# An attention block with a gated MLP on one core: 32-bit back transposes, residual by accumulating DMAs, a fifth shift tile, DMA transposes from SP for tokens 512 to 2047, and a new planned order

## The chip, the cores and the metric

The kernel runs on 1 core of one Trainium2 chip. The metric is the device time in microseconds (us) of one execution; three runs of the kernel before gave 658.18 us as median (658.02 to 658.38).

## The reference, cut to what matters

```python
def reference(A_x, A_wq, A_wk, A_wv, A_wo, B_x, B_w1, B_w2):
    xn = _layernorm(x)                      # x: 2048 tokens x 512
    q = (xn @ wq) as 32 heads of 16;  k = xn @ wk;  v = xn @ wv      # one k and one v for all heads
    p = _softmax(q @ k.T * 16 ** -0.5)      # 32 heads x 2048 x 2048
    s = (p @ v, heads side by side) @ wo    # 2048 x 512
    g = _silu(_silu(xn @ w1) @ w2)          # 2048 x 1792, then 2048 x 512
    return x + s * g
```

B_x of the inputs is not used. Data are bfloat16.

## The kernel before, in words

**Tiles.** The 2048 tokens are four chunks of 512. A score tile is 128 x 512: 64 keys of one chunk, for two heads, against 512 queries, written by four matmuls into one of the eight PSUM banks. A group g (0 to 31) is 64 such tiles (32 blocks of 64 keys, two halves i of a q tile); 2,048 score tiles in all. A score tile is exponentiated in one of two ways:
- by ACT with the Exp function (L1674), one bank or two banks in one instruction, into `pa_sb`;
- by DVE, which writes the bits of an approximate power of two as uint16 (L1042) into `db_sb`, in batches of eight tiles. Three shifted copies of the batch follow in `ds_sb`, each one integer addition over 128 x 4096 (POOL, L1225; in a few cases DVE, L1221), and the four versions are multiplied with differently weighted values `v_sb`, so that their sum approximates the exponential.

PE multiplies each with V (L1303) and adds up in a bank per group. `make_norm` then transposes the bank in 32 x 32 blocks in place (L1320), takes the reciprocal of the sum (L1323), multiplies into `otr_sb` (L1325), and for each pair of groups transposes back, as bfloat16, into `on_sb` (L1335).

**Jobs.** Between the score tiles PE runs jobs that share the banks: q (xn @ wq), h (xn @ w1, tanh on ACT at L761 and a gate on DVE at L762), z (u @ w2, the same two steps into `tmp_sb`) and w (the `on_sb` tiles @ wo). After a w job DVE multiplies with `tmp_sb` in the bank (L814) and adds x from `xr_sb` into `ob_sb` (L817); SP loads `xr_sb` (L825) and stores `ob_sb` (L809). The last four token tiles have a tail of their own (L798 to L803, L1554 to L1568).

**Prologue.** x arrives in 16 tiles of 128 tokens; DVE takes mean and variance (L539, L543), a reciprocal square root and writes `xn_sb` (L568, four slots). PE transposes it through PSUM (L607, by `mk_T`) and DVE copies to `xnT_sb` (L618; the first two tiles by ACT and in halves). For each chunk then follow K (L633 on PE, L651 on DVE into `kt_sb`), a POOL DMA that shifts `kt_sb` for odd groups (L1349), and V (L670, L679). A score tile needs K of its chunk, and its PV needs V of its chunk. DVE tiles start only when K of all 16 token tiles is there (`pick_d`).

**What sets the order.** All instructions are placed at build time by `Planner`, which keeps a clock for every engine and appends the instruction that it picks to that engine's list. Each engine runs its list strictly in order and waits on semaphores. `s_step` picks between an ACT tile and a DVE tile by the work that each engine has ahead; a batch of DVE tiles is only opened while a group has `MARGIN` tiles left. A table of random seeds (`SEEDS`), one for each 6 us stretch of the planner's clock, varies these thresholds. `xn_sb` tile t and t + 4 share a slot, so tile t + 4 is only written when tile t was read. `ports=2` marks operations of DVE and POOL that share a port and are kept apart by semaphores.

Of the kernel before, what the change touches and what calls it, by code (L numbers as in the profile page):

```python
# [8 lines left out]
ALU = mybir.AluOpType  # L9
# [13 lines left out]
SEEDS, STRETCH = [0, 0, 882634, 0, 348373, 328499, 78780, 554384, 89101, 903077, 320169, 0, 878569, 280070, 102111, 381856, 427096, 265022, 0, 740569, 0, 0, 0, 191854, 393933, 374197, 266972, 0, 665170, 0, 882882, 218695, 9227, 955074, 159633, 731624, 518155, 138034, 620799, 357599, 376984, 365473, 457970, 796664, 668429, 641664, 991272, 0, 0, 23990, 593814, 88565, 504692, 394759, 276845, 267858, 882770, 104810, 721623, 135503, 603776, 0, 337714, 100793, 638616, 0, 419715, 752789, 751312, 664693, 308960, 0, 762547, 276261, 218757, 897693, 0, 624478, 290921, 0, 713781, 335568, 417921, 100939, 814701, 0, 180062, 99721, 614963, 258262, 411291, 131548, 802432, 314922, 883804, 569039, 54637, 401726, 110613, 0, 983842, 914345, 0, 0, 0, 0, 0, 0, 0, 0], 6000.0  # L23
# [32 lines left out]
NPA, NDB, NDS, NTM = 27, 3, 4, 4  # L56
MARGIN, MARGIN_END = 17, 20
# [10 lines left out]
MATE = 176.663  # L68
RH, EVR, SC_PRIO, PES = 0, (0, 2, 3), 0, (1, 0)
# [26 lines left out]
class Planner:  # L96

    def __init__(self):
# [7 lines left out]
        self.held = None  # L106
# [3 lines left out]
        self.last2 = {DV: None, PO: None}  # L110

# [68 lines left out]
    def tensor(self, mode, lane, dur, emit, reads, writes, t, after=None, n=8, held=None):  # L180
# [18 lines left out]
        if both or lane == 1:  # L199
            self.held = held  # L200
# [18 lines left out]
    def avail(self, task):  # L219
# [5 lines left out]
        if task.eng == PO and task.ports == 2:  # L225
            for d in self.tasks[DV]:
                if d.ports == 2 and d.gate is None and all(p.op is not None for p in d.preds) and (
                        self.ready(DV, d.reads, d.writes) <= self.clk[PO] + HOLD_PO):
                    return None
# [25 lines left out]
    def finalize(self, new_sem):  # L255
# [96 lines left out]
def bass_recurrent_scan__grouped_kv_mqa__dense_activation_silu__prompt_kernel(  # L352
# [29 lines left out]
    with ExitStack() as es:  # L382
# [59 lines left out]
        xv = xf.rearrange("(t p) d -> p t d", p=P)  # L442

# [53 lines left out]
        pl.add(Task(PO, 1800.0, lambda g: g.memset(kt_sb[0:DH, 1, :], 0.0), [("xn", 3)], [("kt1", c) for c in range(NC)], 3,  # L497
                    gate=lambda: all(xn_task[t].op is not None for t in range(4)), ports=2))
# [99 lines left out]
        def mk_T(tiles, bk=None):  # L598
# [12 lines left out]
            def consume(jb, op):  # L611
# [9 lines left out]
                preds=[xn_task[t] for t in tiles], bk=bk, mode="F")  # L621

# [156 lines left out]
        def mk_z(tt, pace):  # L779
            c, r = divmod(tt, 4)  # L780

            def consume(jb, op):
# [3 lines left out]
                tmp_task[tt] = gated(b, k, 0.25, tmp_sb[:, tt % NTM, :], ("tmp", tt % NTM))  # L786
# [8 lines left out]
        def scaled(tt, b, r=None):  # L795
            k = tt % 2
            if r in EVR:
                ev = pl.add(Task(AC, 490.0, lambda a: a.activation(xn_sb[:, r, :], bank(b), ACT.Copy, scale=0.25),  # L798
                                 [("ps", b)], [("xn", r)], 0))
                fin_task[tt] = Task(DV, 333.0, lambda v: v.tensor_tensor(xn_sb[:, r, :], xn_sb[:, r, :], tmp_sb[:, tt % NTM, :], ALU.mult),  # L800
                                    [("xn", r), ("tmp", tt % NTM)], [("xn", r)], SC_PRIO, [ev, tmp_task[tt]], ports=2)
# [3 lines left out]
                [("ps", b), ("tmp", tt % NTM)], [("fin", k)], 0 if r is None else SC_PRIO, [tmp_task[tt], fin_task.get(tt - 2) if r is None or r - 2 not in EVR else None])  # L805
# [6 lines left out]
        def final(tt, b):  # L812
            k = tt % 2
            t1 = Task(DV, T_P, lambda v: v.scalar_tensor_tensor(  # L814
                out=bank(b), in0=bank(b), scalar=0.25, in1=tmp_sb[:, tt % NTM, :], op0=ALU.mult, op1=ALU.mult),
                [("ps", b), ("tmp", tt % NTM)], [("ps", b)], 0, [tmp_task[tt]])
# [7 lines left out]
        def add_xr(tt):  # L824
# [958 lines left out]
```

## Time and profile before

| | |
|---|---|
| median of three runs | 658.18 us (658.02 to 658.38) |
| span of the profiled execution, first to last instruction | 656.6 us |
| busy: PE, ACT, DVE, POOL | 648.1, 640.4, 639.3, 571.0 us |
| instructions: ACT, DVE, POOL | 1128, 1170, 320 |
| granted TensorE clock | 1.000 |
| DMA share of 16 engines, queue of SP | 6.3% |

The span runs from the first to the last instruction; the page gives no other time for the profiled execution, so 658.18 - 656.6 = 1.6 us is taken as what lies around it. Busy time is the union of the instructions' durations: an instruction that starts while the one before it still drains adds only what is not overlapped, so an engine that shows 100% may still have waited a little between starts. Lines of the kernel are named L followed by the number.

### The profile page before, as it was taken

To read this page: it belongs to the slowest core of one execution; us is meant where nothing else is said; L and a number is where in the kernel's file an instruction comes from. 1 tells how busy PE (TensorE), PEld (TensorE's weight loads), DVE (VectorE), ACT (ScalarE), POOL (GpSimd) and SP (SyncE) were. 2 spreads that over 40 slices of the span, in tenths; PEclk is the share of its full clock that TensorE was granted. 3 is DMA by queue.
4 is the path that set the end of the run, shared out by engine and by line. 5 is a ranking of instruction groups with operands and counts; after the bars stand their busy time and mean duration, and the time that the engine had idled before them with its cause. 6 is when DMAs were issued, how large, how long until landed. Compare 5 with 4: busy or idle time off the path is not lost.

```text
span 656.6 us, 44475 instructions
## 1 busy us (share of the span) xinstructions
PE 648.1 (99%) x22180; PEld 330.7 (50%) x19436; DVE 639.3 (97%) x1170; ACT 640.4 (98%) x1128; POOL 571.0 (87%) x320
## 2 busy tenths in 40 slices
PE   8999999999999999999999999999999999999997
PEld 4445554544455554554555454444555555554444
DVE  8999999999999999999999999999999999999976
ACT  6889999999999999999999999999999999999995
POOL 4038899999998978999999878999999999889991
PEclk9999999999999999999999999999999999999999
DMA  6311111000011100000000010000000000100001
GB/s 177 129 48 42 42 28 29 10 4 10 5 35 28 35 28 4 10 4 6 9 4 12 20 36 26 4 5 9 5 10 4 10 21 20 35 11 5 4 4 34
DMA packets 13641, 15.92 MB, mean 24 GB/s; under 512 B 2320, under 2 KB 12816, under 8 KB 13456
## 3 DMA queue, kind: packets, MB, share of 16 engines
q1 hardware_dynamic: 12976, 12.36, 6.3%
q8 instruction: 162, 2.65, 1.7%
q0 software_dynamic: 192, 0.46, 0.2%
q10 hardware_dynamic: 288, 0.26, 0.1%
q14 instruction: 23, 0.19, 0.1%
HBM read 8.95 MB, written 2.10 MB: 17 GB/s over the span
## 4 chain that ended last, share of the span: by engine, by line
PE 84%; ACT 10%; DVE 3%; POOL 1%; DMA 0%; issue 0%
PE ps L967 28%; PE ps L1303 23%; PE ps L705 20%; PE ps L961 13%; ACT pa_sb L1674 9%; ACT t_sb L761 1%; DVE stats_sb L539 1%; DVE xn_sb L568 1%; PE ps L1514 1%; DVE xnT_sb L618 0%; DMA kt_sb<-kt_sb 0%; POOL qt_sb L501 0%; POOL kt_sb L497 0%; DVE v_sb L679 0%; DVE kt_sb L651 0%
## 5 line engine op out<-in xcount | busy, mean ns | idle before, releaser
L1674 ACT ACTIVATE pa_sb<-ps 128x512 bf16<-128x512 f32 (+1 forms) x1038 | 611.0, 771 | 4.1 <-PE ps L967 3.8
L1225 POOL INT64_ADD ds_sb<-db_sb x300 | 562.1, 1896 | 41.5 <-DVE db_sb L1042 31.9
L1042 DVE TENSOR_SCALAR db_sb<-ps 128x512 uint16<-128x512 f32 x808 | 499.9, 680 | 4.2 <-PE ps L961 2.0
L967 PE MATMUL ps<-qt_sb,kt_sb 64*32 64x512 bf16 x5448 | 470.6, 378 | 1.5 <-DVE v_sb L679 0.8
L1303 PE MATMUL ps<-ds_sb,v_sb 64*32 64x512 bf16 x4848 | 350.5, 377 | 0.0
L1303 PE MATMUL ps<-pa_sb,v_sb 64*32 64x512 bf16 x2480 | 269.9, 377 | 0.5 <-DVE v_sb L679 0.5
L961 PE MATMUL ps<-qt_sb,kt_sb 64*32 64x512 bf16 x2744 | 263.6, 375 | 0.0
L967 PEld LDWEIGHTS ps<-qt_sb,kt_sb 64*32 64x32 bf16 x5448 | 130.4, 89 | 162.8 <-ACT pa_sb L1674 70.6
L1303 PE MATMUL ps<-db_sb,v_sb 64*32 64x512 bf16 x1616 | 210.6, 377 | 0.0
L1303 PEld LDWEIGHTS ps<-ds_sb,v_sb 64*32 64x32 bf16 x4848 | 133.4, 91 | 43.5 <-issue 15.0
L705 PE MATMUL ps<-xnT_sb,w_sb 64*32 64x512 bf16 x1792 | 134.6, 377 | 0.0
L705 PE MATMUL ps<-w_sb,u_sb 64*32 64x512 bf16 x1792 | 133.5, 376 | 0.0
L1303 PEld LDWEIGHTS ps<-pa_sb,v_sb 64*32 64x32 bf16 x2480 | 91.4, 91 | 26.8 <-issue 7.9
L1303 PEld LDWEIGHTS ps<-db_sb,v_sb 64*32 64x32 bf16 x1616 | 66.5, 91 | 15.7 <-issue 5.3
L705 PEld LDWEIGHTS ps<-xnT_sb,w_sb 64*32 64x32 bf16 x1792 | 42.8, 91 | 24.9 <-issue 6.7
L705 PEld LDWEIGHTS ps<-w_sb,u_sb 64*32 64x32 bf16 x1792 | 44.4, 91 | 20.3 <-issue 6.2
L761 ACT ACTIVATE t_sb<-ps 128x512 bf16<-128x512 f32 x72 | 49.1, 682 | 0.0
L762 DVE SCALAR_TENSOR_TENSOR u_sb<-t_sb,ps 128x512 bf16<-128x512 bf16 x56 | 37.9, 677 | 1.0 <-ACT t_sb L761 1.0
L705 PE MATMUL ps<-xnT_sb,wq_sb 64*32 64x512 bf16 x480 | 37.1, 377 | 0.0
L705 PE MATMUL ps<-wo_sb,on_sb 64*32 64x512 bf16 x384 | 30.2, 377 | 0.0
L1320 DVE STREAM_TRANSPOSE ps<-ps 128x512 f32<-128x512 f32 (+1 forms) x33 | 23.2, 706 | 3.6 <-PE ps L1303 3.6
L1349 POOL DMA_DIRECT2D kt_sb<-kt_sb x4 | 2.3, 566 | 21.3 <-DVE rstd_sb L559 7.8
(78 smaller groups left out, 193.0 us busy)
## 6 DMA issues: line engine op xcount, KB each, us to landing
xr_sb<-in_A_x_dram SPq DMA_DIRECT2D x16, 128.0 KB, 2.4
out_dram<-ob_sb SPq DMA_DIRECT2D x16, 128.0 KB, 1.8
w_sb<-in_B_w_dram SPq DMA_DIRECT2D x1, 1792.0 KB, 7.3
w_sb<-in_B_w_dram SPq DMA_DIRECT2D x14, 128.0 KB, 2.1
ds_sb<-in_A_x_dram SPq DMA_DIRECT2D x3, 512.0 KB, 7.1
qt_sb<-qt_sb SPq DMA_DIRECT2D x16, 96.0 KB, 2.2
wq_sb<-in_A_wq_dram SPq DMA_DIRECT2D x1, 512.0 KB, 5.4
wo_sb<-in_A_wo_dram SPq DMA_DIRECT2D x4, 128.0 KB, 2.9
```

What stands on the lines that cost most here:

```text
L539: ts_ = pl.add(Task(DV, 593.0, lambda v, t=t: v.bn_stats(stats_sb[:, t, :], x_tile(t)), [xkey(t)], [("st", t)], 1 + j, gate=(lambda j=j: S ...
L568: xn_task[i] = pl.add(Task(DV, 323.0, lambda v, i=i: v.tensor_scalar(xn_sb[:, i % 4, :], x_tile(i), mv_sb[:, i, 0:1], rstd_sb[:, i:i + 1], ...
L705: h = pe.matmul(bank(b)[32 * j:32 * (j + 1), :], lhsT=lhs(k, rows, 32 * j, 32), rhs=rhs(k, rows), start=first, stop=last, tile_position=(r ...
L761: t1 = Task(AC, T_AF + 0.8333 * NQ, lambda a: a.activation(t_sb[:, k, :], bank(b), ACT.Tanh, scale=scale), [("ps", b)], [("t", k)], 0)
L762: t2 = Task(DV, T_P, lambda v: v.scalar_tensor_tensor(out=dst, in0=t_sb[:, k, :], scalar=1.0, in1=bank(b), op0=ALU.add, op1=ALU.mult), [(" ...
L961: h = pe.add_instruction(mybir.InstMatmult(name=pe.bass.get_next_instruction_name(), engine=mybir.EngineType.PE, ins=[pe.lower_ap(q), pe.l ...
L967: h = pe.matmul(to, lhsT=keys, rhs=q, start=True, stop=True, tile_position=(r0, 32 * j), skip_group_check=True)
L1042: bt.P[k] = pl.add(Task(DV, T_P, lambda v: v.tensor_scalar(db_sb[:, bt.b, k * NQ:(k + 1) * NQ], bank(b), 128.0 * LOG2E, 128.0 * (SHIFT_BET ...
L1225: whole["po"].append(pl.add(Task(PO, T_P64, lambda g: g.int64_add(ds_sb[:, s, :].bitcast(U64), db_sb[:, bt.b, :].bitcast(U64), words), rea ...
L1303: h = pe.matmul(bank(OB)[q:q + 32, :], lhsT=lhs[rows], rhs=rhs[rows], start=s0, stop=s1, tile_position=(64 * l, q), skip_group_check=True)
L1320: t1 = pl.add(Task(DV, (T_TR - 60.0) / parts + 60.0, lambda v, cols=cols: v.transpose(bank(OB)[:, cols], bank(OB)[:, cols]), [("ps", OB)], ...
L1674: op = pl.place(AC, 0.8333 * NQ * n + T_AF, lambda a: a.activation(pa3[:, k0:k1 + 1:max(1, k1 - k0), :], ps3[:, b0:b1 + 1:step, :], ACT.Ex ...
```

## The change

- **Back transposes**: the transpose into `on_sb` reads and writes pairs of bfloat16 as one 32-bit element (256 elements a row in place of 512). `make_norm` writes `otr_sb` in another layout for it, and the readers of `on_sb` take every second column (`on_cols`).
- **Residual**: for token tiles 0 to 11, x is copied to the output by a DMA from HBM to HBM (SP), the multiplication with `tmp_sb` writes `ob_sb`, and a DMA from POOL adds `ob_sb` to the output. The DVE addition is gone for these twelve. The last four tiles keep theirs.
- **DMA transposes**: tokens 512 to 2047 are transposed from `xn_sb` to `xnT_sb` by 48 DMA transposes of 128 x 128 from SP, four for each token tile, that count on one semaphore per tile. The PE transposes and DVE copies of these tokens are gone.
- **Buffers**: `tmp_sb` is now `xn_sb`; `xr_sb`, `fin_sb` and a new `fx_sb` lie in `w1_sb`, once it is no longer read; the room goes to a fifth `ds_sb` tile.
- **Planner**: DVE tiles may start with K of 12 token tiles (`DK`), rank behind the prologue until it is over (`PRO_PRIO`); two DVE tiles that are ready together may become one instruction (`both_passes`); POOL's port operations also give way to gated DVE tasks (`YIELD`); `MARGIN` 17 to 24; new `SEEDS`. Among the other new names, `P_HIGH` keeps a batch from being opened while POOL has much shift work ahead; the score tiles still go to one lane of PE and the PV products to the other.

```diff
-NPA, NDB, NDS, NTM = 27, 3, 4, 4
-MARGIN, MARGIN_END = 17, 20
+NPA, NDB, NDS, NTM = 27, 3, 5, 4
+MARGIN, MARGIN_END = 24, 20
...
+TR32, XBAR, T_TURN = 1, 1, 500.0
+YIELD, W_LATE = 1, 0.0
+DK, PRO_PRIO, ZDMA = 12, 6, 0
...
+        def add_turn(t):
+            cols = slice(t * P, (t + 1) * P)
+            for d in range(NDC):
+                def emit(e, d=d):
+                    return e.dma_start_transpose(xnT_sb[:, d, cols], xn_sb[:, t % 4, d * P:(d + 1) * P])
+                last = d == NDC - 1
+                pl.add(Task(SP, T_TURN, emit, [("xn", t % 4)], [("xnT", t)] if last else [], 0,
+                            [xn_task[t]], dma=1, on_place=(lambda op: t_done.add(t)) if last else None)).ring = f"x{t}"
...
         def final(tt, b):
-            k = tt % 2
+            if tt < NT - 4:
+                t1 = Task(DV, T_P, lambda v: v.scalar_tensor_tensor(
+                    out=ob_sb[:, tt % 4, :], in0=bank(b), scalar=0.25, in1=tmp_sb[:, tt % NTM, :], op0=ALU.mult, op1=ALU.mult),
+                    [("ps", b), ("xn", tt % NTM)], [("ob", tt % 4)], 0, [tmp_task[tt], out_task.get(tt - 4)])
+                fin_task[tt] = t1
+                out_task[tt] = pl.add(Task(PO, T_SWDGE, lambda e: e.dma_start(ov[:, tt, :], ob_sb[:, tt % 4, :], accum_op=ALU.add),
+                                           [("ob", tt % 4)], [("out", tt)], 0, [t1, xr_task[tt]], dma=256 * 1024, on_place=outs.append))
+                return t1,
...
         def add_xr(tt):
+            if tt < NT - 4:
+                xr_task[tt] = pl.add(Task(SP, 60.0, lambda e: e.dma_start(ov[:, tt, :], xv[:, tt, :]),
+                                          (), [("out", tt)], 2, [], dma=256 * 1024))
...
-            mk_T([4 * c, 4 * c + 1])
-            mk_T([4 * c + 2, 4 * c + 3])
+            if XBAR:
+                for t in range(4 * c, 4 * c + 4):
+                    add_turn(t)
...
-            if st["assigned"] < 8 or any(k not in evac_kt or evac_kt[k].op is None for k in range(NKT)):
+            if st["assigned"] < 8 or any(k not in evac_kt or evac_kt[k].op is None for k in range(DK)):
...
+                op = pl.place(DV, one.dur + NQ / 0.96, lambda v: v.tensor_scalar(
+                    db3[:, k0:k1 + 1:k1 - k0, :], ps3[:, b0:b1 + 1:b1 - b0, :], 128.0 * LOG2E, 128.0 * (SHIFT_BETA + 127.0),
...
-                t2_task[oi] = pl.add(Task(DV, (T_TR - 60.0) / parts + 60.0, lambda v, cols=cols: v.transpose(
+                t2_task[oi] = pl.add(Task(DV, (T_TR - 60.0) / parts / (2 if TR32 else 1) + 60.0, lambda v, cols=cols: v.transpose(
+                    on_sb[:, oi % NON, cols].bitcast(FP32), otr_sb[:, oi % 2, cols].bitcast(FP32)) if TR32 else v.transpose(
                     on_sb[:, oi % NON, cols], otr_sb[:, oi % 2, cols]),
```

The counts of the planned instructions, before and after: ACT exponentials of one bank 836 and 844, of two banks 202 and 198 (1,240 tiles in both); DVE tiles 808 in both (798 single instructions and 5 of two after); shifts on POOL 300 and 298, on DVE 3 and 5; PV matmuls 8,944 in both; score tiles that reuse the loaded weights 686 and 633; PE transposes 64 and 16; DVE copies of `xnT_sb` 8 and 2; DMAs on POOL 4 and 16.

Three places show how the order moves. The first is SP's list around the load of w1 (`w_sb<-in_B_w_dram`, 128x4x1792); before:

```order
L445 DMA ds_sb<-in_A_x_dram 128x4x512 x3
L715 DMA qt_sb<-qt_sb 96x512
L445 DMA w_sb<-in_B_w_dram 128x4x1792
L445 DMA w_sb<-in_B_w_dram 128x512 x4
L715 DMA qt_sb<-qt_sb 96x512
```

and SP's list at the same place after the change:

```order
L468 DMA ds_sb<-in_A_x_dram 128x4x512 x3
L756 DMA qt_sb<-qt_sb 96x512
L468 DMA w_sb<-in_B_w_dram 128x4x1792
L659 DMA_TRANSPOSE xnT_sb<-xn_sb 128x128 x48
L468 DMA w_sb<-in_B_w_dram 128x512 x4
L756 DMA qt_sb<-qt_sb 96x512
```

All 48 transposes stand behind the load of w1 and ahead of the first w2 tiles and of the next q copy.

The second is DVE's list in the prologue, with the semaphores that a row waits for (q_ and an engine: that engine's progress; ax and a number: the four DMA transposes of that token tile). Before, where tokens 512 to 1023 are normalized:

```order
L565 SCALAR_TENSOR_TENSOR rstd_sb<-var_sb,rstd_sb 128x4 [waits q_DVE]
L679 TENSOR_TENSOR v_sb<-ps,wj_sb 128x5x8x16 [waits q_PE]
L568 TENSOR_SCALAR xn_sb<-ds_sb,mv_sb,rstd_sb 128x512 [waits q_DVE,q_POOL]
L568 TENSOR_SCALAR xn_sb<-ds_sb,mv_sb,rstd_sb 128x512 x3
L539 BN_STATS stats_sb<-ds_sb 128x6 [waits d12]
L618 COPY xnT_sb<-ps 128x4x256 [waits q_PE] x2
```

and after, from the end of the normalization of tokens 1024 to 1535 to K of tokens 512 to 1023:

```order
L597 SCALAR_TENSOR_TENSOR rstd_sb<-var_sb,rstd_sb 128x4 [waits q_DVE]
L600 TENSOR_SCALAR xn_sb<-ds_sb,mv_sb,rstd_sb 128x512 [waits ax4,q_DVE]
L600 TENSOR_SCALAR xn_sb<-ds_sb,mv_sb,rstd_sb 128x512 [waits ax5]
L600 TENSOR_SCALAR xn_sb<-ds_sb,mv_sb,rstd_sb 128x512 [waits ax6]
L600 TENSOR_SCALAR xn_sb<-ds_sb,mv_sb,rstd_sb 128x512 [waits ax7]
L571 BN_STATS stats_sb<-ds_sb 128x6 [waits d25]
L571 BN_STATS stats_sb<-ds_sb 128x6
L692 TENSOR_SCALAR kt_sb<-ps,part_sb 128x512 [waits q_PE]
```

The copies are gone, and each normalized tile of the next chunk now waits for the DMA transposes of the tile whose slot it takes.

The third is PE's list around K of tokens 512 to 1023 (`xnT_sb,wke_sb`, 32x512, x16). Before, with the PE transposes (`ident,xn_sb`) ahead of it, 20 score tiles stand ahead of K in the whole list:

```order
L607 MATMUL ps<-ident,xn_sb 128x128 x8
L1303 MATMUL ps<-pa_sb,v_sb 32x512 x4
L607 MATMUL ps<-ident,xn_sb 128x128 x8
L1303 MATMUL ps<-pa_sb,v_sb 32x512 x4
L967 MATMUL ps<-qt_sb,kt_sb 32x512 x4
L1303 MATMUL ps<-pa_sb,v_sb 32x512 x4
L961 MATMUL ps<-qt_sb,kt_sb 32x512 x4
L1303 MATMUL ps<-pa_sb,v_sb 32x512 x4
L967 MATMUL ps<-qt_sb,kt_sb 32x512 x4
L1303 MATMUL ps<-pa_sb,v_sb 32x512 x4
L961 MATMUL ps<-qt_sb,kt_sb 32x512 x4
L633 MATMUL ps<-xnT_sb,wke_sb 32x512 x16
```

and after:

```order
L1024 MATMUL ps<-qt_sb,kt_sb 32x512 x4
L1018 MATMUL ps<-qt_sb,kt_sb 32x512 x4
L1024 MATMUL ps<-qt_sb,kt_sb 32x512 x4
L746 MATMUL ps<-xnT_sb,w_sb 32x512 x4
L1018 MATMUL ps<-qt_sb,kt_sb 32x512 x4
L746 MATMUL ps<-xnT_sb,w_sb 32x512 x8
L674 MATMUL ps<-xnT_sb,wke_sb 32x512 x16
L746 MATMUL ps<-xnT_sb,w_sb 32x512 x4
L1024 MATMUL ps<-qt_sb,kt_sb 32x512 x4
L1018 MATMUL ps<-qt_sb,kt_sb 32x512 x4
```

K of the second chunk moved from behind 20 score tiles to behind 30 of the 32 that the first chunk allows in groups 0 and 1; K of the third from behind 36 to behind 44, and K of the fourth from behind 47 to behind 64, of which 8 are DVE tiles.

More of the change, by code (lines that the diff above doesn't have):

```diff
@@ L226, in avail @@
             for d in self.tasks[DV]:
-                if d.ports == 2 and d.gate is None and all(p.op is not None for p in d.preds) and (
-                        self.ready(DV, d.reads, d.writes) <= self.clk[PO] + HOLD_PO):
+                if d.ports == 2 and (d.gate is None or YIELD and self.clk[DV] <= self.clk[PO] + HOLD_PO and d.gate()) and all(
+                        p.op is not None for p in d.preds) and self.ready(DV, d.reads, d.writes) <= self.clk[PO] + HOLD_PO:
                     return None
@@ L309, in finalize @@
                     op.sem, op.val = sems[e], n
+        for e in ENGINES:
+            for op in self.order[e]:
+                if op.ring is not None:
+                    op.val = rings[op.ring][1]
     def run_engine(self, e, handle):
@@ L1247, in pv_half @@
             got, soon, old = {}, INF, INF
+            last = ob_last.get(g)
+            turn = pl.vis(last, PE) if last is not None and last.lane != lane else 0.0
             for i in range(2):
                 for ent in pvq[g][i]:
+                    if ent.lane != lane:
+                        continue
                     c = ent.reads[-1][2]
@@ L1263, in pv_half @@
             return t, got
-        ob = {}
+        ob, ob_last = {}, {}
         def take_ob():
@@ L1305, in emit @@
                 return h
-            pl.tensor("U", 0, MM, emit, sorted(reads, key=str), [("ps", OB)], t, n=4 * len(mm))
+            last = ob_last.get(g)
+            ob_last[g] = pl.tensor("U", lane, MM, emit, sorted(reads, key=str), [("ps", OB)], t, n=4 * len(mm),
+                                   after=last if last is not None and last.lane != lane else None)
             make_shifts()
@@ L1693, in generic_step @@
             now, soon = pl.best(e, t)
+            if now is not None and now[1].slot is not None and both_passes(max(t, now[2]), now[1]):
+                return True
             if now is not None:
```

214 lines of the change are left out of this document (150 added, 64 removed).

## The prediction

> **What bounds the kernel now.** First the busy times of the page and their course over the span, then a table by stage.
>
> ```profile
> PE 648.1 (99%) x22180; PEld 330.7 (50%) x19436; DVE 639.3 (97%) x1170; ACT 640.4 (98%) x1128; POOL 571.0 (87%) x320
> ACT  6889999999999999999999999999999999999995
> 20.00:40.00 20.00, 18.40 (x510) 9.03 (x446) 17.91 (x51) 16.48 (x29) 1.58 (x3) 1.00 0.29 104
> 40.00:640.00 600.00, 599.88 (x21052) 306.65 (x18396) 593.44 (x1021) 599.90 (x1060) 559.39 (x299) 1.00 0.06 17
> 640.00:657.00 17.00, 12.56 (x324) 6.67 (x284) 10.89 (x22) 9.54 (x15) 2.68 (x2) 1.00 0.10 33
> ```
>
> The columns of the last three rows are PE, PEld, DVE, ACT, POOL. From 40 to 640 us ACT shows 599.90 of 600, DVE 593.44, POOL 559.39. So ACT is the bound, with DVE close behind; ACT's idle time lies before 40 and after 640. Whether ACT is really back to back needs its cadence, since its instructions overlap.
>
> ```profile
> L1674 ACT ACTIVATE pa_sb<-ps 128x512 bf16<-128x512 f32 x836 | 446.2, 694 | 2.6 <-PE ps L967 2.4
> L1674 ACT ACTIVATE pa_sb<-ps 128x1024 bf16<-128x1024 f32 x202 | 213.7, 1090 | 1.5 <-PE ps L967 1.4
> L761 ACT ACTIVATE t_sb<-ps 128x512 bf16<-128x512 f32 x72 | 49.1, 682 | 0.0
> 52.31 4.02 ACT L1674 ACTIVATE pa_sb<-ps 128x512 bf16<-128x512 f32 x8
> 56.13 0.69 ACT L761 ACTIVATE t_sb<-ps 128x512 bf16<-128x512 f32 x1
> 11.51 14.23 ACT L1674 ACTIVATE pa_sb<-ps 128x512 bf16<-128x512 f32 x24 [0.50 <-PE ps L967]
> 633.77 13.21 ACT L1674 ACTIVATE pa_sb<-ps 128x1024 bf16<-128x1024 f32 x17
> ```
>
> One bank lasts 694 ns, but eight of them, all of one bank, start between 52.31 and 56.13: 3.82 / 8 = 0.478 us from start to start, and the rest overlaps. The last row is 11 instructions of two banks and 6 of one: (13.21 - 6 x 0.478 - 0.2 for the drain) / 11 = 0.92 us per two banks. The work of ACT is then 836 x 0.478 + 202 x 0.92 + 72 x 0.478 = 619.8 us. It runs from 11.51 to 646.98 us, 635.3 without the drain. So ACT lost 15.5 us after its first exponential. The view of ACT in order of time shows where 3.3 of them are:
>
> ```profile
> 26.45 4.14 ACT L1674 ACTIVATE pa_sb<-ps 128x1024 bf16<-128x1024 f32 x7 [0.71 <-PE ps L967]
> 31.45 1.57 ACT L1674 ACTIVATE pa_sb<-ps 128x512 bf16<-128x512 f32 x3 [0.86 <-PE ps L967]
> 33.73 2.64 ACT L1674 ACTIVATE pa_sb<-ps 128x1024 bf16<-128x1024 f32 x3 [0.70 <-PE ps L967]
> 38.83 8.80 ACT L1674 ACTIVATE pa_sb<-ps 128x512 bf16<-128x512 f32 x16 [1.05 <-PE ps L967]
> ```
>
> The bracket is idle time and what ended it: scores that came late in the prologue. 599.90 leaves 0.1 for the steady part, so some 12.1 us are **hidden waits**, shorter than the overlap of two instructions. After 646.98 comes the tail, 9.6 us.
>
> **The change, part by part.** The sum is made against the profiled execution: span 656.6 us, and 658.18 - 656.6 = 1.6 us around it.
>
> *ACT's own work.* 1,240 tiles before and after, 844 x 0.478 + 198 x 0.92 + 34.4 = 620.0 us: **+0.2**. This is the main point: no part of the change takes work from the bounding engine. What it can gain is ACT's 15.5 lost us and the tail.
>
> *DVE.*
>
> ```profile
> 619.28 10.99 DVE L1042 TENSOR_SCALAR db_sb<-ps 128x512 uint16<-128x512 f32 x18
> L817 DVE TENSOR_TENSOR ob_sb<-ps,xr_sb 128x512 bf16<-128x512 f32 x12 | 8.1, 677 | 0.0
> L618 DVE COPY xnT_sb<-ps 128x1024 bf16<-128x1024 bf16 x6 | 4.0, 680 | 0.5 <-PE ps L607 0.5
> L1335 DVE STREAM_TRANSPOSE on_sb<-otr_sb 128x512 bf16<-128x512 bf16 x15 | 10.5, 702 | 0.0
> L1320 DVE STREAM_TRANSPOSE ps<-ps 128x256 f32<-128x256 f32 x2 | 0.8, 444 | 1.5 <-PE ps L1303 1.5
> L1221 DVE TENSOR_SCALAR ds_sb<-db_sb 128x4096 uint16<-128x4096 uint16 x3 | 3.5, 1222 | 0.0
> ```
>
> Eighteen evictions take 10.99 us, 0.61 from start to start, 0.07 less than their mean of 0.68. By it 12 additions go (12 x 0.60 = 7.2) and 6 copies (3.6). A transpose of 256 32-bit elements is in the trace at L1320, 444 ns against 702: 15 x 0.26 = 3.9, and 0.3 for the two halves in the tail. Two more shifts on DVE cost 2 x 1.15 = 2.3. Two DVE tiles in one instruction are not in the trace: between nothing and one whole eviction saved, 5 x 0 to 0.61; I take the overhead that ACT saves, 2 x 0.478 - 0.92 = 0.04 each, nearly nothing. DVE loses 12.7 us net, all of it beside ACT. It is worth something only where PE waited for DVE to free a bank and so fed ACT late:
>
> ```profile
> PEld ps L967 <- ACT pa_sb L1674: 70.6, 292, 0.5
> PEld ps L967 <- DVE db_sb L1042: 35.7, 165, 0.4
> ```
>
> The waits of the score tiles' weight loads for a bank are 35.7 / 106.3 = 34% DVE's. Of the 12.1 hidden us that is 4.1. DVE stays over 95% busy, so I take three quarters: **-3.1**. The ends are 0 (ACT itself is what frees banks late) and -4.1; past it, all 12.1.
>
> *Prologue.*
>
> ```profile
> 16.50 1.38 DVE L568 TENSOR_SCALAR xn_sb<-ds_sb,mv_sb,rstd_sb 128x512 bf16<-128x512 bf16 x4 [0.76 <-POOL kt_sb L497]
> 17.27 22.11 SPq L445 DMA_DIRECT2D w_sb<-in_B_w_dram  x5
> 19.73 1.05 PE L633 MATMUL ps<-xnT_sb,wke_sb 128*32 128x512 bf16 x16
> 21.51 0.73 DVE L651 TENSOR_SCALAR kt_sb<-ps,part_sb 128x512 bf16<-128x512 f32 x1
> 0.75 0.86 SPq L445 DMA_DIRECT2D ds_sb<-in_A_x_dram  x2
> 50.31 0.52 SPq L715 DMA_DIRECT2D qt_sb<-qt_sb  x1
> w_sb<-in_B_w_dram SPq DMA_DIRECT2D x1, 1792.0 KB, 7.3
> qt_sb<-qt_sb SPq DMA_DIRECT2D x16, 96.0 KB, 2.2
> ```
>
> In the new list the normalized tiles 4 to 7 stand ahead of V and of POOL's fill, so they come at about 14.6 us in place of 16.50. SP then issues w1 (15.4, done at 15.9) and the 48 transposes. No DMA transpose is in the trace. The nearest rows are single DMAs on SP: 0.43 us each for x, 0.52 for the copy inside SBUF, which lands 2.2 us after issue. I take 0.5 per transpose, its end 1.7 after. The far end is a queue that holds each until it has landed, 2.2 each; the near end 0.43. With 0.5, K's inputs are there at 15.9 + 8 + 1.7 = 25.6 us for the second chunk, 33.6 for the third, 41.6 for the fourth. From K's start to scores I count 1.05 + 0.73 + 0.6 for three handovers = 2.4 us: scores at 28.0, 36.0, 44.0. ACT's first 32 tiles (18 single, 7 double) end at 11.5 + 15.0 = 26.5, so it waits 1.5 us plus its hand-over; 14 tiles later 36.0 comes as ACT runs out; 12 ACT tiles after that (8 of the 20 are DVE's) end near 42. That is 4 to 5 us of waits, as before (3.3 shown and about 1 hidden): **0**. Each 0.1 us more per transpose costs 4.8 us, since PE's list holds K of the fourth chunk ahead of everything that follows; DVE waits as well, its next normalized tile standing in its list ahead of statistics, K and V. The w1 transfer fills the same queue until about 22.7 us (7.3 from issue), which the issue of the first chunk's transposes covers. Their PE counterparts (48 transposes, some 3.7 us) and PSUM banks go; PE's list waits for K anyway: 0.
>
> The Trainium skill, "VectorE: DVE Perf Modes", section "The three transpose paths", puts a 128 x 128 bf16 transpose through the DMA crossbar at 1309 ns, against 390 on TensorE. No run here shows it yet. If that were the time per transpose in one queue, the sum would be an estimated 48 x 0.81 = 39 us higher; the same skill, "Advanced Engine Details and Errata", section "X-Bar Transpose (TRN2)", calls such DMAs as fast as regular ones, which leaves the sum as it is.
>
> *Residual.*
>
> ```profile
> L1225 POOL INT64_ADD ds_sb<-db_sb x300 | 562.1, 1896 | 41.5 <-DVE db_sb L1042 31.9 <-PE ps L1303 8.0 <-PE ps L961 1.0
> L1349 POOL DMA_DIRECT2D kt_sb<-kt_sb x4 | 2.3, 566 | 21.3 <-DVE rstd_sb L559 7.8 <-DVE kt_sb L651 7.4 <-DVE mv_sb L543 6.1
> ```
>
> Twelve accumulating DMAs on POOL at 0.57 (the four of L1349) are 6.8 us, two shifts less give back 3.7: +3.1 on POOL, whose 40 idle us between 40 and 640 hide it; without that cover it would be +3.1. An accumulation waits for its product on DVE, and shifts stand behind it, and PV behind those; the fifth shift tile lets more of them be ready. The copies of x from HBM to HBM need the queue only long before. 0.
>
> *Tail.* The two half transposes get 0.14 shorter each, in line: **-0.2**; the rest is as before.
>
> Sum: 656.6 + 0.2 - 3.1 + 0 - 0.2 = 653.5 us of span, and with 1.6 around it **655.1 us**, 0.5% under 658.18. A measurement of this kernel can tell about 0.2%, 1.3 us, from no change.
>
> **Rivals.**
>
> *The transposes are slow* (slower). The price is 48 x (t - 0.5) for a time t of each in SP's queue; from t = 0.59 the time is over 659.5, slower by 0.2%. For it: nothing in the trace shows one, all 48 go through one queue, and three engines wait in line. Against it: plain DMAs issue in 0.43 to 0.52. With t = 0.85 it gives 672, with 2.2 each (far end) 655.1 + 81.6 = 737. At the 1309 ns of the page of the Trainium skill named above it would be an estimated 694.
>
> *The hidden waits stay* (no change). They come from ACT's own bank turnover (70.6 us of the waits) or from the shift to a new order: then only +0.2 - 0.2 is left, 656.9 to 659.5 with a us for a prologue that fits a little better or worse.
>
> *DVE is the bound after all.* Its 593.44 of 600 says it is close. Then the 12.7 us come off whole: 656.6 - 12.7 + 1.6 = 645.5. Against it: ACT's 620.0 + 11.5 + 9.6 = 641.1 would leave it 3 us of waits in all.
>
> **How the numbers follow.** Forecast 0.55 (650 to 656.8), hidden waits stay 0.14, transposes slow 0.26 (half of it, 0.13, between 659.5 and 672, half above), DVE the bound 0.05. Faster is 0.55 + 0.05 = 0.60, same 0.14, slower 0.26. The range runs from 650.0 (655.1 less the last quarter of DVE's share, 1.0, and the four us of prologue waits) to 672 (t = 0.85); it leaves out 0.13 + 0.05. For the faster cases alone the range is 645 to 656.8.
>
> **What would show it.** In the profile after, the view of SP: from the start of the first transpose to the last one's issue about 24 us, and the first K of tokens 512 to 1023 on PE near 25.6 us. ACT's exponentials again 0.48 and 0.92 apart, ending about 3 us sooner than 646.98; DVE's busy time near 627 us; POOL's DMAs of the residual near 0.57 each, with little idle time before the shifts that follow. It is wrong if K of the later chunks comes late and ACT is idle for long before 60 us (the transposes), if ACT ends no sooner with the prologue as planned (the hidden waits), or if ACT's idle time nearly vanishes (DVE).

## The result, and the profile after

The changed kernel takes **702.15 us** (median of four runs, 701.61 to 702.65) against 658.11 (658.02 to 658.38) before: 1.0668 of it, 95% interval 1.0655 to 1.0681. It is 6.7% slower; 655.1 was forecast. The profiled execution took 702.08 us with a span of 700.3, 43.7 more than before.

First the busy times of the page and the rows of ACT and of the TensorE clock over the span:

```profile
PE 653.4 (93%) x22131; PEld 342.1 (49%) x19600; DVE 630.2 (90%) x1149; ACT 641.0 (92%) x1132; POOL 577.2 (82%) x330
ACT  6443199999999999999999999999999999999996
PEclk9766599999999999999999999999999999999999
```

ACT's work is what it was (641.0 against 640.4 busy), but it is busy 40, 40, 30 and 10% of the second to fifth slice. A slice is 17.5 us, so the loss lies between 17.5 and 87.5 us. By stage (columns PE, PEld, DVE, ACT, POOL, then the clock):

```profile
20.00:40.00 20.00, 5.34 (x80) 1.20 (x56) 3.96 (x12) 6.37 (x10) 0.00 (x0) 0.70 0.23 60
40.00:60.00 20.00, 6.80 (x164) 3.01 (x134) 6.18 (x21) 7.37 (x12) 0.55 (x1) 0.67 0.15 32
60.00:80.00 20.00, 9.45 (x228) 4.83 (x192) 7.40 (x11) 6.29 (x11) 2.41 (x2) 0.67 0.14 31
640.00:690.00 50.00, 50.00 (x1676) 27.28 (x1444) 43.41 (x70) 50.00 (x78) 38.60 (x21) 1.00 0.02 5
```

From 20 to 80 us every engine of these columns is idle for half of the time or more, so none of them is short of capacity there. Near the end ACT is full again. The groups of ACT's exponentials, apart by shape, give the size:

```profile
L1780 ACT ACTIVATE pa_sb<-ps 128x512 bf16<-128x512 f32 x844 | 448.4, 704 | 46.3 <-PE ps L1024 45.8 <-PE ps L1018 0.4
L1780 ACT ACTIVATE pa_sb<-ps 128x1024 bf16<-128x1024 f32 x198 | 208.8, 1101 | 1.5 <-PE ps L1024 1.4
```

The idle time ahead of them is 46.3 + 1.5 = 47.8 us against 2.6 + 1.5 = 4.1 before: +43.7, the whole difference of the spans. In the chain of work that ended last, by engine, SP's queue has 6% of the span, some 42 us:

```profile
PE 90%; SPq 6%; DVE 2%; DMA 1%; ACT 0%; issue 0%
```

These are SP's list in order of time, the durations of the transposes with their time to landing, and K of the three later chunks on PE:

```profile
15.18 0.37 SPq L468 DMA_DIRECT2D w_sb<-in_B_w_dram  x1
15.60 63.96 SPq L659 DMA_TRANSPOSE xnT_sb<-xn_sb  x48
79.61 2.00 SPq L468 DMA_DIRECT2D w_sb<-in_B_w_dram  x4
```

```profile
L659 SPq DMA_TRANSPOSE xnT_sb<-xn_sb x48: 1222/1232/2376, 15.6 to 78.3; - x48
...
DMA to landing us min/median/max: 2.3/2.4/7.2
```

```profile
37.65 1.90 PE L674 MATMUL ps<-xnT_sb,wke_sb 128*32 128x512 bf16 x16 [13.00 <-DMA xnT_sb<-xn_sb]
59.17 1.90 PE L674 MATMUL ps<-xnT_sb,wke_sb 128*32 128x512 bf16 x16 [12.67 <-DMA xnT_sb<-xn_sb]
80.70 1.90 PE L674 MATMUL ps<-xnT_sb,wke_sb 128*32 128x512 bf16 x16 [11.25 <-DMA xnT_sb<-xn_sb]
```

A transpose holds SP for 1.232 us (median; minimum 1.222), and the 48 take 63.96 us where 24 were forecast. One lands 2.4 us (median) after its issue starts, while the next starts 63.96 / 48 = 1.33 us after the one before: the queue does not wait for the landing, it is the issue that is slow. K, whose starts were forecast from 25.6, comes at 37.65, 59.17 and 80.70, and PE waits 13.00, 12.67 and 11.25 us for it. ACT's view shows the same three holes:

```profile
40.18 1.08 ACT L1780 ACTIVATE pa_sb<-ps 128x512 bf16<-128x512 f32 x2 [13.81 <-PE ps L1024]
63.50 1.08 ACT L1780 ACTIVATE pa_sb<-ps 128x512 bf16<-128x512 f32 x2 [14.80 <-PE ps L1024]
85.04 1.09 ACT L1780 ACTIVATE pa_sb<-ps 128x512 bf16<-128x512 f32 x2 [14.77 <-PE ps L1024]
```

### The profile page after: what moved, and what is told of

Read it like the earlier page. It is cut to its first block, busy times and chain, and to the rows that moved or that the text cites. A ratio compares the mean times of both kernels' runs of the same rounds, so it can differ in the third digit from the quotient of the medians.

```text
span 700.3 us, 44688 instructions
## 1 busy us (share of the span) xinstructions
PE 653.4 (93%) x22131; PEld 342.1 (49%) x19600; DVE 630.2 (90%) x1149; ACT 641.0 (92%) x1132; POOL 577.2 (82%) x330
## 4 chain that ended last, share of the span: by engine, by line
PE 90%; SPq 6%; DVE 2%; DMA 1%; ACT 0%; issue 0%
PE ps L1371 29%; PE ps L1024 27%; PE ps L746 19%; PE ps L1018 12%; SPq L659 6%; DMA xnT_sb<-xn_sb 1%; PE ps L1733 1%; PE ps L674 1%; PE ps L711 1%; ACT pa_sb L1780 0%; DVE db_sb L1102 0%; PE ps L1593 0%; DVE stats_sb L571 0%; DVE w_sb L841 0%; DVE xn_sb L600 0%
## 5 line engine op out<-in xcount | busy, mean ns | idle before, releaser
L1780 ACT ACTIVATE pa_sb<-ps 128x512 bf16<-128x512 f32 (+1 forms) x1042 | 611.5, 779 | 47.8 <-PE ps L1024 47.3
L1024 PE MATMUL ps<-qt_sb,kt_sb 64*32 64x512 bf16 x5660 | 477.5, 380 | 1.6 <-ACT pa_sb L1780 1.2
L1371 PE MATMUL ps<-pa_sb,v_sb 64*32 64x512 bf16 x2480 | 258.7, 379 | 1.0 <-ACT pa_sb L1780 0.5
L1018 PE MATMUL ps<-qt_sb,kt_sb 64*32 64x512 bf16 x2532 | 244.6, 378 | 1.6 <-ACT pa_sb L1780 1.5
L1024 PEld LDWEIGHTS ps<-qt_sb,kt_sb 64*32 64x32 bf16 x5660 | 135.6, 90 | 160.7 <-ACT pa_sb L1780 65.8
L1371 PE MATMUL ps<-db_sb,v_sb 64*32 64x512 bf16 x1616 | 179.8, 377 | 0.0
L746 PE MATMUL ps<-w_sb,u_sb 64*32 64x512 bf16 x1792 | 130.4, 377 | 0.0
L1371 PEld LDWEIGHTS ps<-pa_sb,v_sb 64*32 64x32 bf16 x2480 | 85.8, 91 | 25.9 <-issue 7.4
L1371 PEld LDWEIGHTS ps<-db_sb,v_sb 64*32 64x32 bf16 x1616 | 58.3, 91 | 14.6 <-issue 4.8
L674 PE MATMUL ps<-xnT_sb,wke_sb 128*32 128x512 bf16 (+2 forms) x80 | 6.9, 486 | 36.9 <-DMA xnT_sb<-xn_sb 36.9
L600 DVE TENSOR_SCALAR xn_sb<-ds_sb,mv_sb,rstd_sb 128x512 bf16<-128x512 bf16 x16 | 6.1, 410 | 28.9 <-DMA xnT_sb<-xn_sb 28.8
```

What stands on the lines that cost most here:

```text
L674: h = pe.matmul(bank(b)[32 * j:32 * (j + 1), 0:n], lhsT=wke_sb[:, dc, 32 * j:32 * (j + 1)], rhs=xnT_sb[:, dc, ka * P:kb * P], start=dc == ...
L746: h = pe.matmul(bank(b)[32 * j:32 * (j + 1), :], lhsT=lhs(k, rows, 32 * j, 32), rhs=rhs(k, rows), start=first, stop=last, tile_position=(r ...
L1018: h = pe.add_instruction(mybir.InstMatmult(name=pe.bass.get_next_instruction_name(), engine=mybir.EngineType.PE, ins=[pe.lower_ap(q), pe.l ...
L1024: h = pe.matmul(to, lhsT=keys, rhs=q, start=True, stop=True, tile_position=(r0, 32 * j), skip_group_check=True)
L1371: h = pe.matmul(bank(OB)[q:q + 32, :], lhsT=lhs[rows], rhs=rhs[rows], start=s0, stop=s1, tile_position=(64 * l, q), skip_group_check=True)
L1780: op = pl.place(AC, 0.8333 * NQ * n + T_AF, lambda a: a.activation(pa3[:, k0:k1 + 1:max(1, k1 - k0), :], ps3[:, b0:b1 + 1:step, :], ACT.Ex ...
```

## The experiments

**Theory A**: SP's time in these transposes is the whole loss, and it is paid per instruction. Rivals: **B**, it is paid per 128 x 128 block; **C**, the new order or another part of the change loses the time. Times are medians; beside each experiment the kernel before ran on the same chip (medians 658.2 to 659.1 us), and the ratio stands against these runs.

**One transpose for each token tile.** Four blocks of a tile in one instruction, all else in place:

```diff
-  return e.dma_start_transpose(xnT_sb[:, d, cols], xn_sb[:, t % 4, d * P:(d + 1) * P])
+  return e.dma_start_transpose(xnT_sb[:, :, cols], xn_sb[:, t % 4, :]) if d == 0 else None
```

> Edit: the planned order of every engine stays as in the changed kernel, but one DMA transpose of 128 x 512 takes the place of the four of 128 x 128 of a token tile, 12 in place of 48. In the changed kernel each of the 48 held SP for 1.275 us. Theory A (SP pays per instruction): 12 x 1.3 = 16 us of issue in place of 64, K of the later chunks comes as planned or sooner, ACT's 43 us of waits before 100 us go, and the time is 653 to 660 us. Theory B (SP pays per 128 x 128 block, whatever the instruction): each takes 4 x 1.275 = 5.1 us, K starts near 37.6, 59.2 and 80.7 us again, and the time stays 699 to 705 us. Theory C (not SP but something else in the new order holds the prologue): no change either, though SP is done early.

Measured: **658.97 us**, ratio 1.0017 (1.0006 to 1.0028). SP's list, the duration of one, K's starts and ACT's groups:

```profile
15.64 21.93 SPq L659 DMA_TRANSPOSE xnT_sb<-xn_sb  x12
```

```profile
L659 SPq DMA_TRANSPOSE xnT_sb<-xn_sb x12: 1190/1310/2607, 15.6 to 35.0; - x12
...
DMA to landing us min/median/max: 2.4/3.9/7.3
```

```profile
24.62 1.05 PE L674 MATMUL ps<-xnT_sb,wke_sb 128*32 128x512 bf16 x16
32.20 1.05 PE L674 MATMUL ps<-xnT_sb,wke_sb 128*32 128x512 bf16 x16
39.89 1.05 PE L674 MATMUL ps<-xnT_sb,wke_sb 128*32 128x512 bf16 x16
```

```profile
L1780 ACT ACTIVATE pa_sb<-ps 128x512 bf16<-128x512 f32 x844 | 447.3, 701 | 3.4 <-PE ps L1024 3.3
L1780 ACT ACTIVATE pa_sb<-ps 128x1024 bf16<-128x1024 f32 x198 | 208.4, 1099 | 0.8 <-PE ps L1024 0.8
```

A transpose of 128 x 512 holds SP 1.310 us, one of 128 x 128 1.232: four times the data at 6% more. B falls, and so does C as the cause of the 43 us, since the order of every engine is that of the changed kernel. ACT's idle time is 4.2 us, as before the change (4.1).

**Two for each token tile.**

```diff
+  return e.dma_start_transpose(xnT_sb[:, d:d + 2, cols], xn_sb[:, t % 4, d * P:(d + 2) * P]) if d % 2 == 0 else None
```

> Edit: the order of the changed kernel, with two DMA transposes of 128 x 256 for each token tile, 24 in all. Theory A (SP pays about 1.3 us per instruction): 24 x 1.3 = 31 to 33 us of issue against 21.9 with 12 and 64.0 with 48. By the price of the prediction, one us of time for each us of issue past some 22 us, the time is 659 + 10 = 667 to 672. Theory B (per block): 64 us of issue, 702.

Measured: 671.77 us, ratio 1.0202 (1.0169 to 1.0234), within the 667 to 672 of A; SP's stretch of 34.04 us is a us over A's 31 to 33.

```profile
L659 SPq DMA_TRANSPOSE xnT_sb<-xn_sb x24: 1243/1247/2131, 15.7 to 48.5; - x24
...
DMA to landing us min/median/max: 2.4/3.0/8.8
```

```profile
15.73 34.04 SPq L659 DMA_TRANSPOSE xnT_sb<-xn_sb  x24
```

**Plain copies at the same places.**

```diff
-  return e.dma_start_transpose(xnT_sb[:, d, cols], xn_sb[:, t % 4, d * P:(d + 1) * P])
+  return e.dma_start(xnT_sb[:, d, cols], xn_sb[:, t % 4, d * P:(d + 1) * P])
```

> Edit: the 48 DMAs from xn_sb to xnT_sb are plain copies of the same 128 x 128 blocks, without the transposition (so K, V, q and h are computed from data that are not transposed); the order of every engine is that of the changed kernel. It asks what the prediction's world would have been: a DMA that SP issues in about 0.5 us. If the issue time of the transposes is the whole loss (theory A and B alike): SP's 48 copies take 21 to 26 us, K of the second chunk starts near 25.6 us, and the time is what was forecast with t = 0.5, 655 us, within 652 to 659; if DVE's slack brings nothing, 657 to 659. If other parts of the change or of its order lose time too (theory C): over 662 us, up to 702.

Measured: 672.02 us, ratio 1.0208 (1.0193 to 1.0223). This is outside what A expected, though no transpose is left. It lies in the range that was given to C (over 662), but one transpose per tile, with the same order and the same other parts, is at 658.97, so C does not follow.

```profile
15.61 34.09 SPq L659 DMA_DIRECT2D xnT_sb<-xn_sb  x48
```

```profile
L659 SPq DMA_DIRECT2D xnT_sb<-xn_sb x48: 599/601/1974, 15.6 to 49.1; - x48
...
  DVE xn_sb L600: 8.7, 6
...
DMA to landing us min/median/max: 1.8/1.9/6.8
```

The copy takes 0.601 us in place of 0.5, and SP's 34.09 us are more than 48 x 0.601 = 28.8. The missing 5.2 look like a loop at first: `xn_sb` has four slots, DVE may write the next tile only when the copies of the tile four earlier have landed, and it waits 8.7 us for them. But SP never waits for DVE in return. It comes to token tiles 8 and 12 at 26.59 and 38.06 us, and DVE wrote them 2.7 us earlier:

```profile
23.45 0.41 DVE L600 TENSOR_SCALAR xn_sb<-ds_sb,mv_sb,rstd_sb 128x512 bf16<-128x512 bf16 x1 [2.59 <-DMA xnT_sb<-xn_sb]
34.90 0.73 DVE L600 TENSOR_SCALAR xn_sb<-ds_sb,mv_sb,rstd_sb 128x512 bf16<-128x512 bf16 x2
38.06 0.60 SPq L659 DMA_DIRECT2D xnT_sb<-xn_sb  x1
42.58 1.97 SPq L659 DMA_DIRECT2D xnT_sb<-xn_sb  x1
```

Tiles 9 to 11 and 13 to 15 were ready earlier still. The 5.2 us are the 0.043 us that lie between one copy and the next (47 x 0.043 = 2.0) and four copies that last 1.07 to 1.97 us in place of 0.60 (3.2). Each of the four overlaps a transfer of the instruction queue (from 15.45, 28.92, 36.03 and 42.52 us); no run shows whether that is the cause. Only with one transpose per tile does SP pause for DVE's tiles, 1.3 and 1.9 us. Times and SP's busy stretch go together, whatever the instruction:

| kernel, same order on all other engines | instructions x median | the stretch on SP | rest of it | time |
|---|---|---|---|---|
| one transpose per tile | 12 x 1.310 = 15.7 | 21.93 | 6.2 | 658.97 |
| two per tile | 24 x 1.247 = 29.9 | 34.04 | 4.1 | 671.77 |
| plain copies | 48 x 0.601 = 28.8 | 34.09 | 5.2 | 672.02 |
| changed kernel | 48 x 1.232 = 59.1 | 63.96 | 4.8 | 702.15 |

From the first to the third row the time grows by 13.05 us for 12.16 of SP, from the third to the fourth by 30.13 for 29.87: one for one.

**The transposes alone**, put into the kernel before (the code below leaves out `add_turn`, which is that of the change):

> Edit: the kernel before, with the 48 DMA transposes from SP in place of the transposes on TensorE and no other part of the change; its planner counts 500 ns for each and so puts K of chunks two to four behind 32, 42 and 56 score tiles. If the transposes are the whole loss: SP is busy with them until near 80 us, K starts near 37, 59 and 80 us, ACT waits 40 to 48 us more than in the kernel before, and the time is 695 to 710 us. If the loss needs the other parts of the change: under 680 us.

```diff
-            mk_T([4 * c, 4 * c + 1])
-            mk_T([4 * c + 2, 4 * c + 3])
+            for t in range(4 * c, 4 * c + 4):
+                add_turn(t)
```

Measured: 713.57 us, ratio 1.0840 (1.0823 to 1.0856). SP and the exponentials of one bank:

```profile
17.39 63.68 SPq L632 DMA_TRANSPOSE xnT_sb<-xn_sb  x48
```

```profile
L1688 ACT ACTIVATE pa_sb<-ps 128x512 bf16<-128x512 f32 x932 | 494.1, 713 | 47.9 <-PE ps L981 47.0 <-PE ps L1317 0.3
```

SP is taken for 63.68 us, nearly as long as in the changed kernel (63.96), and ACT is idle 47.9 us ahead of these, so no other part of the change is needed for the loss. The time is 3.6 us past the upper end expected, in an order that was made anew. ACT's idle time ahead of all its exponentials grew by 49.5 - 4.1 = 45.4 us, within the 40 to 48 expected, and its busy time by 8.0 (648.4 against 640.4): the new order gives ACT 932 + 2 x 158 = 1,248 tiles in place of 1,240, with 44 fewer double exponentials.

**All transposes on TensorE**, with the rest of the change kept:

> Edit: the changed kernel with XBAR = 0: all tokens are transposed on TensorE again and copied by DVE, and all other parts of the change stay; the planner makes a new order with the same seeds. If the DMA transposes are the whole loss: K of the second chunk near 20 to 22 us, ACT's waits before 100 us back at about 6 us, and the time is 655 to 661 us (the seeds were not drawn for this order, which can cost a us or two). If the rest of the change loses time as well: over 664 us.

```diff
-TR32, XBAR, T_TURN = 1, 1, 500.0
+TR32, XBAR, T_TURN = 1, 0, 500.0
```

Measured: 663.99 us, ratio 1.0090 (1.0074 to 1.0107). 38 of the 44 us are gone, but the time lies between the two ranges and so decides for neither theory.

```profile
L1780 ACT ACTIVATE pa_sb<-ps 128x512 bf16<-128x512 f32 x956 | 502.4, 702 | 7.2 <-PE ps L1024 6.2 <-PE ps L1371 0.2 <-PE ps L1018 0.2
L1780 ACT ACTIVATE pa_sb<-ps 128x1024 bf16<-128x1024 f32 x138 | 148.0, 1102 | 0.9 <-PE ps L1024 0.9
```

ACT's idle time is 7.2 + 0.9 = 8.1 us, 3.9 more than with one transpose per tile, and it does 112 more single and 60 fewer double exponentials. The seeds were not drawn for this order; whether that or the rest of the change costs the 6 us, this run can't tell.

**Whether any one engine holds the steady part.** With one transpose per tile the prologue is close to the forecast, and still the time is 658.97, not 655.1. The next runs keep that kernel's order and leave out a part of the work of one engine or of several.

> Edit: the kernel with one transpose per token tile (658.97 us), its order unchanged; of the 72 gate operations on DVE (L803) the last 54 work on 256 of 512 columns (the other columns of h and z are left as they were). DVE loses 54 x 0.267 = 14.4 us more. The step of the prediction that failed said that 34% of ACT's hidden waits (11.5 us here between 100 and 640) are DVE's: by it the time falls by 3 to 4 us, to 655 to 656. Theory N (DVE's slack is worth nothing, since PE and ACT set the end): 658.2 to 659.5. If DVE were the bound after all: 645 to 648.

> Edit: the same kernel and order; of the 72 tanh of ACT (L802) the last 68 work on 256 of 512 columns (the other columns are left as they were). ACT's cadence of 0.478 us falls to about 0.29 there, 68 x 0.185 = 12.6 us less. If ACT alone sets the end, as the prediction read the profile: 646 to 649 us. If PE is as full as ACT (theory P: PE stands at 98% busy and is 94% of the chain that ended last): at most a third of it, 655 to 658.5.

> Edit: the same kernel and order; in 207 of the units of four PV matmuls from ds_sb on PE 256 of 512 columns are multiplied (the other columns get no such term). A unit takes PE some 0.11 us of the span (645 us / 22131 matmuls x 4), so about 207 x 0.055 = 11 us less. If ACT alone sets the end: at most the hidden waits shrink, 656 to 659 us. Theory P (PE is as full as ACT): ACT's hidden waits go and the time falls by 3 to 8 us, to 651 to 656; if PE alone sets the end, 647 to 649.

> Edit: the cuts of ACT's tanh and of PE's PV matmuls together, same order. If ACT alone sets the end: as with ACT's cut alone, 646 to 649. Theory P: the two cuts together bring more than the sum of each alone, 645 to 649, while each alone stays over 651. If something else holds both (banks that come free late, the order): over 653.

> Edit: the kernel with one transpose per token tile, its order unchanged, with the cuts of ACT's tanh (12.6 us) and of DVE's gate operations (14.4 us) together. ACT's cut alone brought 1.4 us, DVE's none, and with ACT's cut the score tiles waited most for banks of DVE. Theory Q (the two engines pace each other, since PE's list holds their tiles in a fixed order and a wait for a bank of the one delays the tiles of the other): the two cuts together bring 6 to 11 us, 648 to 653. If PE or something else holds both: 656 to 658.

> Edit: the same with the cut of PE's PV matmuls (11 us) as well, so that ACT, DVE and PE are relieved by 11 to 14 us each. Theory Q with PE as the third of the engines that pace each other: 644 to 650, and more than 2 us under the run with ACT and DVE alone. If PE has room: the same as that run within 1.5 us. If the hold is neither of the three (POOL's shifts, 88% busy): 655 to 658.

> Edit: the order of the kernel with one transpose per token tile, with the cuts of ACT (12.6 us), DVE (14.4 us) and PE (11 us), and with 14 of POOL's 298 shifts, one in twenty, on 2048 of 4096 elements (14 x 0.93 = 13 us; the other halves keep older values). Theory Q4 (ACT, DVE, PE and POOL are all full in the steady part, POOL 98.9 of 100 us between 100 and 300, and pace one another): under the 654.17 us of the cut of three by 4 to 8 us, 646 to 650. If POOL has room: 653 to 655.

> Edit: the kernel with one transpose per token tile, same order, with POOL's 14 half shifts alone (13 us less on POOL). If POOL is the bound that the prediction overlooked: 645 to 651 us. Theory Q4 (four engines pace one another, so that one alone brings nothing): 657 to 659.5.

The edits for DVE, ACT, PE and POOL, in this order and shortened (the combined runs take several of them):

```diff
+            m = NQ if tcount[0] <= 18 else 256; t2 = Task(DV, T_P, lambda v: v.scalar_tensor_tensor(
+                out=dst[:, 0:m], in0=t_sb[:, k, 0:m], scalar=1.0, in1=bank(b)[:, 0:m], op0=ALU.add, op1=ALU.mult),
...
+            w = NQ if tcount[0] <= 4 else 256; t1 = Task(AC, T_AF + 0.8333 * NQ, lambda a: a.activation(
+                t_sb[:, k, 0:w], bank(b)[:, 0:w], ACT.Tanh, scale=scale), [("ps", b)], [("t", k)], 0)
...
+        half = lambda ds, mm: 256 if ds and not any(x[3] or x[4] for x in mm) and next(count) % 5 == 4 else NQ
+            def emit(pe, w=half(ds, mm)):
+                        h = pe.matmul(bank(OB)[q:q + 32, 0:w], lhsT=lhs[rows], rhs=rhs[rows, 0:w], start=s0, stop=s1,
...
+            lambda g: (lambda c: g.int64_add(ds_sb[:, s, 0:c].bitcast(U64), db_sb[:, bt.b, 0:c].bitcast(U64), words))(
+                2048 if next(turns) % 20 == 19 else 4096),
```

| cut | us off each, as worked out | time | ratio to before (95%) |
|---|---|---|---|
| none (one transpose per tile) | | 658.97 | 1.0017 (1.0006 to 1.0028) |
| DVE | 14.4 | 659.81 | 1.0025 (1.0015 to 1.0035) |
| ACT | 12.6 | 657.60 | 0.9982 (0.9970 to 0.9993) |
| PE | 11 | 660.11 | 1.0024 (1.0015 to 1.0034) |
| POOL | 13 | 661.32 | 1.0032 (1.0018 to 1.0045) |
| ACT, PE | | 657.06 | 0.9984 (0.9973 to 0.9995) |
| ACT, DVE | | 657.10 | 0.9977 (0.9965 to 0.9989) |
| ACT, DVE, PE | | 654.17 | 0.9924 (0.9901 to 0.9948) |
| all four | | 655.51 | 0.9945 (0.9928 to 0.9961) |

No single cut brings more than (1.0017 - 0.9982) x 658.2 = 2.3 us; those of DVE, PE and POOL bring nothing. ACT, DVE and PE together bring 0.0093 x 658.2 = 6.1 us, and all four 4.7. Only the cuts of ACT, of ACT with PE and of ACT with DVE end inside a range that was given to a theory: the first in that of P, the other two where something else holds the engines. The cuts of DVE, PE, POOL and of all four lie 0.3 to 1.8 us above the nearest range, that of ACT, DVE and PE 0.8 us below it.

The us of the second column were worked out from rows, not measured. The busy time of the engine falls by less: from one transpose per tile to its single cut, ACT's by 6.2 us, DVE's by 7.9, POOL's by 11.8, PE's by 0.5 (645.5 to 645.0). So for PE it isn't shown that the cut relieved it.

The stretch from 100 to 640 us of the kernel without a cut, with ACT's, and with all four:

```profile
100.00:640.00 540.00, 540.00 (x19040) 289.80 (x16832) 529.10 (x906) 539.97 (x960) 516.72 (x283) 1.00 0.07 14
```

```profile
100.00:640.00 540.00, 539.96 (x19092) 310.78 (x16873) 529.62 (x909) 536.22 (x962) 517.14 (x283) 1.00 0.07 14
```

```profile
100.00:640.00 540.00, 538.86 (x19122) 294.22 (x16902) 521.52 (x908) 536.26 (x963) 505.24 (x283) 1.00 0.07 14
```

ACT shows 3.78 us of idle time with its own cut, and 3.74 with all four, in a stretch where it had 0.03. So ACT alone does not set the end, and by the single cuts neither does DVE or POOL. PE is not ruled out in this way: it shows 540.00 of 540, its cut may not have relieved it, and added to those of ACT and DVE it brings 657.10 - 654.17 = 2.9 us. Theory Q4, that the four pace each other, expected 646 to 650 for all four and 657 to 659.5 for POOL alone, and fails by both numbers (655.51 and 661.32). What stays open is what holds them: each list has a fixed order with waits between the engines, and an instruction that ends sooner at a few places may only wait longer at the next hand-over, but no run shows that mechanism. No version that beats the kernel before was found; of those that compute the whole reference, one transpose per tile comes nearest.

## Why the prediction was wrong, step by step

- **What bounds the kernel**: half right. ACT does the 844 and 198 exponentials that were counted, and its busy time is all but unchanged (641.0 against 640.4). But a cut that was worked out as 12.6 us of its work brings 2.3, so "ACT is the bound" was too strong.
- **Prologue, the time of a transpose**: this is the step that failed, "I take 0.5 per transpose". It takes 1.232 us, more than double: the plain DMAs of the trace before, at 0.43 to 0.52, were no measure for the issue of a transpose. The price given, 48 x (t - 0.5), then makes 35 of the 47 us by which the forecast missed.
- **Prologue, SP's stretch**: also too small. 48 x 0.5 = 24 us left out what comes on top of the usual instruction, 4 to 6 us in all four rows of the table of SP's stretches: the 0.04 us between two, the few that last longer and, with one per tile, SP's waits for DVE's tiles. So the copies, at t = 0.601, cost 13 us against one transpose per tile, where the price would give 4.8. With plain copies in place of the transposes the time is 672.02, so an issue as fast as theirs would not have given the 655.1.
- **Prologue, all else**: right as far as the runs show. With SP done nearly as planned (21.93 us for 24, one transpose per tile), K came at 24.62, 32.20 and 39.89 where 25.6, 33.6 and 41.6 for its inputs were worked out, and ACT's waits were the 4.2 us that made this term 0. The price of one us per us of SP held over 42 us, though it starts at 22 us of SP or less, not at 24: some 2 us more of the miss. The load of w1 delays the first four transposes (7.2 down to 3.5 us to landing in the changed kernel, 7.3 to 3.7 with one per tile), and K of the second chunk still came a us sooner than worked out.
- **DVE, -3.1**: wrong as well; nothing of it shows. The relief is there (transposes of 256 elements, busy 630.2 in place of 639.3, where 627 was worked out), but with the prologue in order the time is 1.0017 of before, and a further cut on DVE changed nothing. This makes 658.97 - 655.1 = 3.9 us of the miss. That PE's weight loads wait for banks of DVE 34% of the time says who came last, not what time comes back when it is faster.
- **Residual, 0**: right in the sum, too low in the row. POOL's accumulating DMAs take 0.87 us where 0.57 was taken, and POOL's busy time grew by 6.2, not 3.1; it is not seen in the time with one transpose per tile.

```profile
L859 POOL DMA_DIRECT2D out_dram<-ob_sb x12: 754/868/1150, 256.3 to 614.6; - x12
```

- **Tail, -0.2**: right. The last exponential ends at 676.63 + 14.49 = 691.12, and the span 9.2 us later, against 9.6 before.

```profile
676.63 14.49 ACT L1780 ACTIVATE pa_sb<-ps 128x1024 bf16<-128x1024 f32 x16
```

- **The rivals**: "the transposes are slow" is what happened, beyond the 672 at which the range ended. With that loss taken out, "the hidden waits stay" fits: 658.97 lies in its 656.9 to 659.5. "DVE is the bound" fails, since DVE's cut brings nothing. The estimate from the Trainium skill, "VectorE: DVE Perf Modes", section "The three transpose paths" (1309 ns for a 128 x 128 transpose), was 694 us; the 1.232 us measured on SP is 6% under that figure. A 128 x 512 transpose at 1.310 shows that it is not a price per block here. The other page of the Trainium skill, "Advanced Engine Details and Errata", section "X-Bar Transpose (TRN2)", which calls such DMAs as fast as regular ones, does not hold for their issue: 1.232 against 0.601 for the plain copy at the same place.

## What to carry to other kernels

Ask first what one instruction of a new kind costs the queue that issues it, times their number, and put as much as it takes into each: here 12 instructions in place of 48 gave back 43 us. If no trace shows that cost, it is the widest term of the sum, and the range has to reach its far end. Waits of a nearly full engine say who came last; only a cut on the chip says what freeing that engine is worth.

## What was not expected of the hardware

- The time of a DMA transpose on SP goes by the instruction: 1.232 us for 128 x 128, 1.247 for 128 x 256, 1.310 for 128 x 512, with landing after 2.4, 3.0 and 3.9 us.
- Where PE waits here, its granted clock is lower: 0.67 to 0.70 from 20 to 80 us, where it was 1.00 in the kernel before from 20 us on. The 48 matmuls of K of the later chunks take 606 to 634 ns, against 379 (median) in the kernel before and with one transpose per tile; the first row is that of one per tile.

```profile
L674 PE MATMUL ps<-xnT_sb,wke_sb x48: 379/379/390, 24.6 to 40.6; 128*32 128x512 bf16 x48
L674 PE MATMUL ps<-xnT_sb,wke_sb x48: 606/634/634, 37.6 to 82.0; 128*32 128x512 bf16 x48
```

It seems to cost little here: from the third to the last row of the table of SP's stretches the time lies 0.3 us above one for one.
